# Soft mixture of experts behind pooled attention: scores by paired heads, one reader per output buffer, second engines in the last run

## The chip, the cores and the metric

One core of a Trainium2 chip runs the whole program. The time is device microseconds of one execution; lower is better. Three runs of the kernel before are known.

## The reference

```python
# attention: 8 batches, 8 heads, 576 tokens, head size 64; keys and values averaged over 8 neighbours
k_p, v_p = mean of 8 keys, mean of 8 values              # 72 per batch
attn = softmax(q @ k_p.T / 8) @ v_p                      # heads side by side: x is 4608 x 512
# dense layer with a rational function
h = x @ w_in                                             # 4608 x 2048
g = (a0 + a1*h + a2*h*h + a3*h*h*h) / (1 + |b0|*|h| + |b1|*h*h + 1e-6)
x = g @ w_out                                            # 4608 x 512
# soft mixture of 8 experts with 4 slots each
logits = x @ phi                                         # 4608 x 32
slot = softmax(logits, over tokens).T @ x                # 32 x 512
slot_out[e] = relu(slot[e] @ w1[e]) @ w2[e]              # 512 -> 1024 -> 512, each expert its 4 slots
out = softmax(logits, over slots) @ slot_out             # 4608 x 512
```

`w_in` and `w_out` arrive as float64, the rest as float32. The output is float32, 9.44 MB.

## The kernel before

**The work.** The 4608 tokens are 36 tiles of 128. Four tiles make a run, nine runs (r = 0 to 8) the dense part. `attention(t)` makes one tile of x: the scores of all eight heads against the 72 pooled keys (L364), VectorE's maximum and subtraction (L370, L374), the exponential on ScalarE, sums and normaliser, a multiplication (L389), eight transposes (`pt`, L398), the product with the pooled values (`av`, L409), and the split into a rounded part `xh` (ScalarE, L413) and the rest `xl` (VectorE, L414). `pooling(b)` sums a batch's keys into `kp` and its values into `vp` (L330, L337).

**Scores.** `kp` is [128, 4, 72]: head pair p, the even head in partitions 0 to 63 and the odd one in 64 to 127. Each head is a matmul of its own, of 64 rows and 72 columns, eight a tile; the even heads go to one PSUM buffer `sc`, the odd ones to another.

**Dense part.** `dense(r, p)` does two of the 16 F-tiles for the run's 512 tokens: h in one PSUM buffer of two banks, as three products of rounded words for each 128 rows of the contraction (L484 to L486). Then S=h*h, A=a3*h+a2 and U=|h| on ScalarE (L495, L497, L498); A=A*S on GpSimd (L499, tasks at L500), A=a1*h+A on VectorE (L502); S=b1*U+b0 and U=U*S on GpSimd (L505, L507); logarithm and negative exponential on ScalarE make the reciprocal r (L510, L513), in the single PSUM buffer `r`; three VectorE instructions (L514, L516, L518) refine it and multiply. TensorE adds this pair's logits (`lg`, L530) and transposes (`gp`, L534), and a copy puts the result into `gt` (L543). In run 0 the two multiplications may go to VectorE, and S to ScalarE. In the last run only the last pair is done in halves. `routing(r)` keeps the softmax over tokens running and adds the run's slot sums (`pss`, L593).

**Weights.** `win(f)` and `wout(f)` turn float64 words into float32 (`words`: one ScalarE instruction, L427, and three of VectorE, L428, L430, L432) during run 0; `win` splits them into `wh` (L441, L442), `wout` also makes w_out times phi by transposes (L454) into the buffer `wo` and a product (L463). So the logits need no x after the dense layer, and w_out is applied to the 32 slots alone at the end.

**End.** `experts()` issues 72 loads of 512 KB as buffers come free: eight of w_out, then w1 and w2. `tail()` applies w_out to the slots (L654), spreads them (`pi`, L663), multiplies by w1 (`l`, L708) and w2 (`lo`, L737), regroups (`pg`, L776), and combines: for each pair of tiles two products into one two-bank PSUM buffer `po` (L788), one half copied by ScalarE (L791), the other by VectorE (L793), both with the normaliser of the softmax over slots as scale, and one store of 512 KB (L795). Eighteen such pairs are there.

**The order.** Nothing is issued in the order of the code. Every instruction group is a task of `Plan` with an engine, a cost in the planner's units, a key (its due time) and buffers; some have a second engine as `alt`. `Plan.run` simulates the engines and gives out, at each step, the task that can start first, ties by key. HEAD, FIRST and RUN are the due times of the runs, SLACK the distance it keeps between a producer and TensorE. Engines then run their lists in order; semaphores hold what isn't ready.

## Time and profile before

| | us |
|---|---|
| three runs | 904.78, 908.6, 910.22; median 908.6 |
| the profiled execution | 908.17, of it 906.4 in the span |
| TensorE busy (share of the span) | 823.0 (91%) |
| VectorE, ScalarE, GpSimd busy | 622.7, 605.9, 523.5 |
| transferred | 97.60 MB |

The trace names TensorE PE (its weight loads PEld), VectorE DVE, ScalarE ACT, GpSimd POOL and the engine that issues the transfers SP. An fp32 matmul shows as two instructions. A line in square brackets gives the idle time ahead of an instruction and what ended it. The granted clock (PEclk) is 1.00 at TensorE's 2.4 GHz and 0.50 at its 1.2 GHz level. By stage: 0 to 55 us the first attention tiles, to 143 run 0, to 781 the h products of the other runs, to 811 the end of the last run, to 868 the experts, then the combine and its stores.

### The profile page before, as it was taken

To read this page: it belongs to the slowest core of one execution; us is meant where nothing else is said; L and a number is where in the kernel's file an instruction comes from. 1 tells how busy PE (TensorE), PEld (TensorE's weight loads), DVE (VectorE), ACT (ScalarE), POOL (GpSimd) and SP (SyncE) were. 2 spreads that over 40 slices of the span, in tenths; PEclk is the share of its full clock that TensorE was granted. 3 is DMA by queue.
4 is the path that set the end of the run, shared out by engine and by line. 5 is a ranking of instruction groups with operands and counts; after the bars stand their busy time and mean duration, and the time that the engine had idled before them with its cause. 6 is when DMAs were issued, how large, how long until landed. Compare 5 with 4: busy or idle time off the path is not lost.

```text
span 906.4 us, 15125 instructions
## 1 busy us (share of the span) xinstructions
PE 823.0 (91%) x5950; PEld 582.0 (64%) x5950; DVE 622.7 (69%) x978; ACT 605.9 (67%) x908; POOL 523.5 (58%) x333
## 2 busy tenths in 40 slices
PE   3778859799999999999999999999999999679987
PEld 3567637676777677677677767767777776433321
DVE  5888898946777777867887777758677667631023
ACT  2558757747888787788777868878877787731023
POOL 3225242856777778668866958667676766800000
PEclk9999869789999999999999999999999999869975
DMA  9694332240012100200130111000000443749947
GB/s 315 252 331 130 125 121 96 77 126 13 25 39 71 33 25 27 91 25 13 39 102 12 39 51 56 25 1 25 1 2 1 135 144 107 232 166 357 417 183 278
DMA packets 34151, 97.60 MB, mean 108 GB/s; under 512 B 3872, under 2 KB 4128, under 8 KB 34080
## 3 DMA queue, kind: packets, MB, share of 16 engines
q1 hardware_dynamic: 34080, 96.63, 31.1%
q8 instruction: 47, 0.77, 0.3%
q14 instruction: 24, 0.20, 0.1%
HBM read 82.99 MB, written 13.63 MB: 107 GB/s over the span
## 4 chain that ended last, share of the span: by engine, by line
PE 74%; DVE 12%; ACT 8%; DMA 2%; issue 2%; POOL 1%; SPq 0%; DVEq 0%; ACTq 0%; POOLq 0%
PE h L484 14%; PE h L486 13%; PE h L485 13%; PE gp L534 7%; PE av L409 4%; PE pss L593 4%; PE lg L530 4%; PE pt L398 3%; PE lo L737 3%; PE sc L364 3%; PE po L788 2%; DVE a L502 2%; PE l L708 2%; DVE r L516 2%; DVE u L514 1%
## 5 line engine op out<-in xcount | busy, mean ns | idle before, releaser
L484 PE MATMUL h<-xh,wh 128*128 128x512 f32 x576 | 249.5, 433 | 16.9 <-DVE a L502 8.6
L499 POOL TENSOR_TENSOR a<-a,s 128x1024 f32<-128x1024 f32 (+1 forms) x69 | 163.4, 2369 | 123.3 <-ACT a L497 112.9
L486 PE MATMUL h<-xh,wh 128*128 128x512 f32 x576 | 232.1, 403 | 0.5 <-POOL wh L442 0.3
L485 PE MATMUL h<-xl,wh 128*128 128x512 f32 x576 | 231.3, 402 | 0.0
L514 DVE SCALAR_TENSOR_TENSOR u<-u,r 128x512 f32<-128x512 f32 x144 | 98.2, 682 | 109.0 <-ACT r L513 105.3
L507 POOL TENSOR_TENSOR u<-u,s 128x1024 f32<-128x1024 f32 (+1 forms) x70 | 165.0, 2358 | 6.4 <-ACT s L504 1.2
L484 PEld LDWEIGHTS h<-xh,wh 128*128 128x128 f32 x576 | 111.4, 193 | 45.2 <-DVE a L502 12.3
L486 PEld LDWEIGHTS h<-xh,wh 128*128 128x128 f32 x576 | 111.0, 193 | 28.3 <-POOL wh L442 2.2
L485 PEld LDWEIGHTS h<-xl,wh 128*128 128x128 f32 x576 | 112.0, 195 | 18.1
L543 ACT ACTIVATE gt<-gp 128x512 f32<-128x512 f32 x143 | 79.8, 597 | 49.4 <-PE gp L534 47.9
L516 DVE SCALAR_TENSOR_TENSOR r<-a,abt,r 128x512 f32<-128x512 f32 x144 | 107.9, 749 | 0.0
L502 DVE SCALAR_TENSOR_TENSOR a<-h,abt,a 128x1024 f32<-128x1024 f32 (+1 forms) x73 | 92.2, 1264 | 20.1 <-POOL a L499 19.9
L518 DVE SCALAR_TENSOR_TENSOR a<-u,r 128x512 f32<-128x512 f32 x144 | 98.5, 684 | 4.3
L513 ACT ACTIVATE r<-s 128x512 f32<-128x512 f32 x144 | 86.8, 603 | 20.7 <-DVE a L518 19.8
L505 POOL TENSOR_SCALAR s<-u,gb 128x1024 f32<-128x1024 f32 (+1 forms) x71 | 84.4, 1188 | 16.3 <-DVE a L499 9.8
L498 ACT ACTIVATE u<-h 128x1024 f32<-128x1024 f32 (+1 forms) x73 | 73.7, 1011 | 26.1 <-PE h L486 25.7
L510 ACT ACTIVATE s<-u,cc 128x1024 f32<-128x1024 f32 (+1 forms) x73 | 83.2, 1140 | 6.9 <-POOL u L507 6.7
L497 ACT ACTIVATE a<-h,abt 128x1024 f32<-128x1024 f32 (+1 forms) x73 | 87.3, 1195 | 0.0
L534 PE MATMUL gp<-ident,a 128*128 128x128 f32 x576 | 84.0, 285 | 1.9 <-ACT cTs L587 1.1
L495 ACT ACTIVATE s<-h 128x1024 f32<-128x1024 f32 (+1 forms) x73 | 73.5, 1009 | 17.8 <-PE h L486 17.7
L534 PEld LDWEIGHTS gp<-ident,a 128*128 128x128 f32 x576 | 63.6, 143 | 22.0 <-issue 16.8
L389 POOL TENSOR_TENSOR at<-at,st 128x576 f32<-128x576 f32 x35 | 41.1, 1176 | 33.3 <-DVE st L383 29.7
(123 smaller groups left out, 1060.8 us busy)
## 6 DMA issues: line engine op xcount, KB each, us to landing
wx<-in_w SPq DMA_DIRECT2D x64, 512.0 KB
...
```

Source lines behind the costliest of these rows:

```text
L484: p_.matmul(o, w[:, 0, k], xh[r].t[:, k], start=(k == 0), stop=False)
L485: p_.matmul(o, w[:, 0, k], xl[r].t[:, k], start=False, stop=False)
L486: p_.matmul(o, w[:, 1, k], xh[r].t[:, k], start=False, stop=(k == 3))
L497: op("ACT", t_act(n, 1, 2), lambda fl=fl: a_.activation(out=fl(A), in_=fl(h), func=AF.Identity, scale=a3, bias=a2), [pt_(h), abt], [pt_(A) ...
L499: mul = lambda eng, fl=fl: eng.tensor_tensor(out=fl(A), in0=fl(A), in1=fl(S_), op=ALU.mult)
L502: op("DVE", t_dve(n, 1), lambda fl=fl: v_.scalar_tensor_tensor(out=fl(A), in0=fl(h), scalar=a1, in1=fl(A), op0=ALU.mult, op1=ALU.add), [pt ...
L507: mul = lambda eng, fl=fl: eng.tensor_tensor(out=fl(U), in0=fl(U), in1=fl(S_), op=ALU.mult)
L513: op("ACT", t_act(512, 0), lambda f=f, q=q: a_.activation(out=q.t, in_=S_.t[:, f], func=AF.Exp, scale=-1.0), [(S_, f)], [q], c + 10)
L514: op("DVE", t_dve(512), lambda f=f, q=q: v_.scalar_tensor_tensor(out=U.t[:, f], in0=U.t[:, f], scalar=QC, in1=q.t, op0=ALU.add, op1=ALU.mult),
L516: op("DVE", t_dve(512, 1), lambda f=f, q=q: v_.scalar_tensor_tensor(out=q.t, in0=A.t[:, f], scalar=a0, in1=q.t, op0=ALU.add, op1=ALU.mult) ...
L518: op("DVE", t_dve(512), lambda f=f, q=q: v_.scalar_tensor_tensor(out=A.t[:, f], in0=U.t[:, f], scalar=-2.0, in1=q.t, op0=ALU.add, op1=ALU. ...
L534: p_.transpose(pt.t[:, j, f, :], A.t[:, f, o : o + 128], ident)
```

## The change

- Scores: `kp` becomes block-diagonal, [128, 4, 144], zeroed once by GpSimd; key sums go to a buffer `ks` and two ScalarE copies put them into the blocks. One matmul of 128 rows and 144 columns makes both heads of a pair, four a tile, and `sc[0]` holds pairs 0 and 1. `av` reads `a` in the new order.
- Start and run 0: other due times, the queries of the first four tiles loaded first, all of run 0's multiplications on GpSimd (seven were on VectorE), six of its S on ScalarE instead of two, the weight transposes into `att` or `gt` instead of their own buffer.
- Last run: the last two pairs in halves; from pair 4 on the multiplications may go to VectorE, S to ScalarE, and r may take a `wk` buffer; A=a3*h+a2 may go to VectorE in all pairs; the copies of `gt` of the last two pairs too. The planner puts eight A (six whole, two halves) and one multiplication on VectorE there.
- Experts: items 28 and 29 are four half loads, three into query buffers and one into a score buffer; later items may use key and attention buffers. What is multiplied stays the same.
- Combine: the normaliser multiplies the 32 weights of each token ahead of their transposes (one VectorE instruction for each group of runs). Even pairs of tiles have one copy of 1024 columns, odd ones two PSUM buffers with a copy each, on whichever engine the planner finds free, without a scale.

```diff
-HEAD, FIRST, RUN = 30.0, 105.0, 75.0
+HEAD, FIRST, RUN = 27.6, 105.03, 75.0
...
-LAT, SLACK = 0.12, 0.6
+FINE, EITHER = 2, 4
+RW, GD, AD = 4, 6, 0
+A1, A1S = 26.91, 19.0
...
+E0 = 12
+LAT, SLACK = 0.12, 0.86
...
-                        s0 = max(s0, c[0] + LAT)
+                        s0 = max(s0, c[0] + LAT if c[0] else 0.0)
...
-                      ("t", 2, 512), ("wo", 1, 512)):
+                      ("t", 2, 512), ("ks", 1, 144)):
...
-    kp = [fixed([128, 4, SP], f"kp{i}", np_=2) for i in range(2)]
+    kp = [fixed([128, 4, 2 * SP], f"kp{i}", np_=2) for i in range(2)]
...
+        op("POOL", 0.75, lambda i=i: g_.memset(kp[i].t, 0.0), [], [kp[i]], -94)
...
-            return HEAD + 25 + 21.0 * j
+            return HEAD + A1 + A1S * j
...
-            o = kp[b % 2]
-            op("DVE", 1.35, lambda t=t, o=o, i=i: v_.tensor_reduce(out=o.t[:, 2 * i : 2 * i + 2, :], in_=t.t, axis=AX.X, op=ALU.add),
-               [], [t, (o, i)], key, alt=[("POOL", 2.8, lambda t=t, o=o, i=i: tree(t.t, o.t[:, 2 * i : 2 * i + 2, :]), True)] if b != 1 else ())
+            o = buf("ks", [128, 2, SP], "ks")
+            op("DVE", 1.35, lambda t=t, o=o: v_.tensor_reduce(out=o.t, in_=t.t, axis=AX.X, op=ALU.add),
+               [], [t, o], key, alt=[("POOL", 2.8, lambda t=t, o=o: tree(t.t, o.t), True)] if b > 1 or b == 0 and E0 & 8 else ())
+            for par in range(2):
+                rr = slice(64 * par, 64 * par + 64)
+                op("ACT", 0.33, lambda o=o, i=i, par=par, rr=rr: a_.activation(out=kp[b % 2].t[rr, 2 * i : 2 * i + 2, SP * par : SP * par + SP], in_=o.t[rr], func=AF.Copy),
+                   [o], [(kp[b % 2], i)], key + 0.1)
...
-        dma_in(q, lambda: q.t, qT[t], k0 - 30, 128 * 512 * 4)
+        dma_in(q, lambda: q.t, qT[t], (k0 if t > 3 else -8.2 + 0.1 * t) - 30, 128 * 512 * 4)
...
-                    for par in range(2):
-                        rr = slice(64 * par, 64 * par + 64)
-                        p_.matmul(sc[par].t[t0:t1, SP * p : SP * p + SP], q.t[rr, p, t0:t1], kp[bb % 2].t[rr, p, :], start=True, stop=True)
...
-        op("PE", 0.6 * len(sp_), scores, [q] + [kp[x % 2] for x in batches], sc, k0, also=[st, e])
+                    p_.matmul(sc[p // 2].t[t0:t1, 2 * SP * (p % 2) : 2 * SP * (p % 2) + 2 * SP], q.t[:, p, t0:t1], kp[bb % 2].t[:, p, :], start=True, stop=True)
...
+        op("PE", 1.0 + 0.2 * (len(sp_) - 1), scores, [q] + [kp[x % 2] for x in batches], sc, k0, also=[st, e])
...
-                        p_.matmul(av.t[64 * par : 64 * par + 64, p, t0:t1], vp[bb % 2].t[:, c : c + 64], a.t[:, par, p, t0:t1], start=True, stop=True)
+                        p_.matmul(av.t[64 * par : 64 * par + 64, p, t0:t1], vp[bb % 2].t[:, c : c + 64], a.t[:, p // 2, 2 * (p % 2) + par, t0:t1], start=True, stop=True)
...
-        wt = buf("wo", [128, 4, 128], "wt")
+        wt = buf(["att", "gt"], [128, 4, 128], "wt")
...
-        subs = [(0, 1), (1, 2)] if r == NR - 1 and p == NPAIR - 1 else [(0, 2)]
+        subs = [(0, 1), (1, 2)] if r == NR - 1 and p >= NPAIR - FINE else [(0, 2)]
+        either = r == 0 or r == NR - 1 and p >= EITHER
...
-            op("ACT", t_act(n, 1, 2), lambda fl=fl: a_.activation(out=fl(A), in_=fl(h), func=AF.Identity, scale=a3, bias=a2), [pt_(h), abt], [pt_(A)], c)
+            op("ACT", t_act(n, 1, 2), lambda fl=fl: a_.activation(out=fl(A), in_=fl(h), func=AF.Identity, scale=a3, bias=a2), [pt_(h), abt], [pt_(A)], c,
+               alt=[("DVE", t_dve(n, 1), lambda fl=fl: v_.tensor_scalar(out=fl(A), in0=fl(h), scalar1=a3, scalar2=a2, op0=ALU.mult, op1=ALU.add), False)] if r == NR - 1 and p >= AD else ())
...
-               alt=[("DVE", t_dve(n), lambda mul=mul: mul(v_), True)] if r == 0 else ())
+               alt=[("DVE", t_dve(n), lambda mul=mul: mul(v_), True)] if (E0 & 1 if r == 0 else either) else ())
...
-               [pt_(U), gb], [pt_(S_)], c + 4, alt=[wa] if r == 0 else ())
+               [pt_(U), gb], [pt_(S_)], c + 4, alt=[wa] if (E0 & 4 if r == 0 else either) else ())
...
-               alt=[("DVE", t_dve(n), lambda mul=mul: mul(v_), True)] if r == 0 else ())
+               alt=[("DVE", t_dve(n), lambda mul=mul: mul(v_), True)] if (E0 & 2 if r == 0 else either) else ())
...
-            q = buf("r", [128, 512], "r")
+            q = buf(["r", "wk"] if r == NR - 1 and p >= RW else "r", [128, 512], "r")
...
-               alt=[("DVE", 0.69, lambda gt=gt, gv=gv: v_.tensor_copy(gt.t[:, :, sl], gv()), False)] if r == NR - 1 and p == NPAIR - 1 else ())
+               alt=[("DVE", 0.69, lambda gt=gt, gv=gv: v_.tensor_copy(gt.t[:, :, sl], gv()), False)] if r == NR - 1 and p >= GD else ())
...
+            if 28 <= n < 30:
+                halves = [buf("q", [128, 512], "wx"), buf("q" if n == 28 else "at", [128, 512], "wx")]
+                w, e, k = it
+                v = lambda b: b.t if len(b.t.shape) == 2 else b.t.rearrange("p a h s -> p (a h s)")[:, 0:512]
+                for h, b in enumerate(halves):
+                    src = (w1 if w == 1 else w2)[e, k][:, 512 * h : 512 * h + 512]
+                    op("SP", 0.06, lambda b=b, src=src, v=v: nc.sync.dma_start(out=v(b), in_=src), [], [b], key, nbytes=128 * 2048)
+                ew[it] = (halves, lambda h, halves=halves, v=v: v(halves[h]))
+                continue
...
-                b = buf(["kv", "att"] if n < 8 else ["w", "gt", "A"], [128, 2, 512], "wx")
+                b = buf(["kv", "att"] if n < 8 else ["w", "gt", "A", "kv", "att"], [128, 2, 512], "wx")
...
+            op("DVE", t_dve(n), lambda c3=c3, cm=cm, nt=nt: v_.tensor_tensor(out=c3(), in0=c3(), in1=cm(2).rearrange("p (a o) -> p a o", o=1).to_broadcast([128, nt, 32]), op=ALU.mult),
+               [csum], [cr], kk, port=True)
...
-            po = buf("h", [128, 2, 512], "po", np_=2)
...
-            def comb(n=n, po=po):
+            po = [buf("h", [128, 2, DM], "po")] if n % 2 == 0 else [buf(["wk", "r"], [128, DM], "po") for _ in range(2)]
+            to = lambda i, po=po: po[0].t[:, i] if len(po) == 1 else po[i].t
...
+            def comb(n=n, to=to):
...
-                    p_.matmul(po.t[:, i], cTs.t[rr, n // 2, :], so4.t[rr, :], start=True, stop=True)
...
-            op("PE", 0.95, comb, [(cTs, n // 2), so4], [po], kk)
-            op("ACT", 0.69, lambda n=n, o=o, po=po: a_.activation(out=o.t[:, 0, :], in_=po.t[:, 0], func=AF.Copy, scale=csum.t[:, 2, 2 * n : 2 * n + 1]),
-               [(po, 0), csum], [(o, 0)], kk)
-            op("DVE", 0.75, lambda n=n, o=o, po=po: v_.tensor_scalar(out=o.t[:, 1, :], in0=po.t[:, 1], scalar1=csum.t[:, 2, 2 * n + 1 : 2 * n + 2], scalar2=None, op0=ALU.mult),
-               [(po, 1), csum], [(o, 1)], kk)
+                    p_.matmul(to(i), cTs.t[rr, n // 2, :], so4.t[rr, :], start=True, stop=True)
...
+            op("PE", 0.95, comb, [(cTs, n // 2), so4], po, kk)
+            for i in range(len(po)):
+                w = 2 * DM // len(po)
+                oo = lambda i=i, o=o, po=po: o.t if len(po) == 1 else o.t[:, i]
+                op("ACT", t_act(w), lambda i=i, oo=oo, po=po: a_.activation(out=oo(), in_=po[i].t, func=AF.Copy), [po[i]], [o if len(po) == 1 else (o, i)], kk,
+                   alt=[("DVE", t_dve(w), lambda i=i, oo=oo, po=po: v_.tensor_copy(oo(), po[i].t), False)])
```

**The order of the engines.** First VectorE in run 0, ahead of the `xl` of the 4th tile, before and after. `wi` and `wo` are words of w_in and w_out, `st` and `at` the softmax of a tile, L428 to L432 are L437 to L441 after.

```order
L428 TENSOR_SCALAR wi<-wi 128x512
L430 SCALAR_TENSOR_TENSOR wi<-raw,wi 128x512
L432 SCALAR_TENSOR_TENSOR wi<-raw,wi 128x512
L428 TENSOR_SCALAR wo<-wo 128x512
L430 SCALAR_TENSOR_TENSOR wo<-raw,wo 128x512
L370 TENSOR_REDUCE st<-sc 128x4
L374 TENSOR_TENSOR at_66<-sc,st 128x4x72 x2
L432 SCALAR_TENSOR_TENSOR wo<-raw,wo 128x512
L428 TENSOR_SCALAR wi<-wi 128x512
L430 SCALAR_TENSOR_TENSOR wi<-raw,wi 128x512
L432 SCALAR_TENSOR_TENSOR wi<-raw,wi 128x512
L414 SCALAR_TENSOR_TENSOR xl<-av,xh 128x4x128
```

```order
L379 TENSOR_REDUCE st<-sc 128x4 x2
L383 TENSOR_TENSOR at_66<-sc,st 128x4x72
L441 SCALAR_TENSOR_TENSOR wo<-raw,wo 128x512
L383 TENSOR_TENSOR at_66<-sc,st 128x4x72
L437 TENSOR_SCALAR wi<-wi 128x512
L439 SCALAR_TENSOR_TENSOR wi<-raw,wi 128x512
L423 SCALAR_TENSOR_TENSOR xl<-av,xh 128x4x128
```

Two `wi` and one or two `wo` conversions that stood ahead of the last `xl` are behind it now.

GpSimd at the end of the last run, before and after (`a`, `s`, `u` are A, S, U; x2 are two like rows; L499, L505, L507 are L510, L516, L518 after):

```order
L499 TENSOR_TENSOR a<-a,s 128x1024
L505 TENSOR_SCALAR s<-u,gb 128x1024
L507 TENSOR_TENSOR u<-u,s 128x1024
L499 TENSOR_TENSOR a<-a,s 128x512 x2
L505 TENSOR_SCALAR s<-u,gb 128x512 x2
L667 MEMSET sp 128x1024
L507 TENSOR_TENSOR u<-u,s 128x512 x2
L684 COPY selv<-sels 128x128
```

```order
L516 TENSOR_SCALAR s<-u,gb 128x1024
L518 TENSOR_TENSOR u<-u,s 128x1024
L510 TENSOR_TENSOR a<-a,s 128x512
L516 TENSOR_SCALAR s<-u,gb 128x512
L518 TENSOR_TENSOR u<-u,s 128x512
L510 TENSOR_TENSOR a<-a,s 128x512
L516 TENSOR_SCALAR s<-u,gb 128x512
L518 TENSOR_TENSOR u<-u,s 128x512
L687 MEMSET sp 128x1024
L510 TENSOR_TENSOR a<-a,s 128x512 x2
L516 TENSOR_SCALAR s<-u,gb 128x512
L518 TENSOR_TENSOR u<-u,s 128x512 x2
```

Pair 6 comes in halves of 512 columns as pair 7 does, and one of their `s` is no longer GpSimd's.

VectorE in the combine, with the semaphores that its copies wait for (DMAHW are transfers), before and after:

```order
L793 TENSOR_SCALAR o<-po,csum 128x512 [waits DMAHW3_49,DMAHW2_49,Activation_49]
L793 TENSOR_SCALAR o<-po,csum 128x512 [waits DMAHW4_49,Activation_49]
L793 TENSOR_SCALAR o<-po,csum 128x512 [waits DMAHW5_49,Activation_49]
L793 TENSOR_SCALAR o<-po,csum 128x512 [waits DMAHW6_49,Activation_49]
L793 TENSOR_SCALAR o<-po,csum 128x512 [waits DMAHW7_49,Activation_49]
```

```order
L818 COPY o<-po 128x512 [waits DMAHW2_49,PE_49]
L818 COPY o<-po 128x512 [waits DMAHW4_49,PE_49]
L818 COPY o<-po 128x512 [waits DMAHW5_49,DMAHW2_49,PE_49]
L818 COPY o<-po 128x512 [waits DMAHW7_49,DMAHW4_49,PE_49]
L818 COPY o<-po 128x512 [waits DMAHW6_49,DMAHW1_49,PE_49]
```

The copies waited for ScalarE (Activation); they wait for TensorE (PE) now. There were 18 of them, there are 9.

## Rows read from the trace of the kernel before

**Rows 1.** Page, the chain that ended last: share of the span by engine.
```profile
PE 74%; DVE 12%; ACT 8%; DMA 2%; issue 2%; POOL 1%; SPq 0%; DVEq 0%; ACTq 0%; POOLq 0%
```

**Rows 2.** Windows by stage: busy us per engine (instructions), granted clock, DMA share and GB/s.
```profile
core 0: us, PE busy (x) PEld busy (x) DVE busy (x) ACT busy (x) POOL busy (x), PEclk, DMA share, GB/s
90.00:130.00 40.00, 31.40 (x190) 23.83 (x192) 35.44 (x56) 26.95 (x43) 15.85 (x12) 0.74 0.32 101
...
450.00:525.00 75.00, 72.49 (x578) 54.93 (x580) 57.33 (x93) 58.95 (x88) 57.06 (x37) 1.00 0.16 47
...
750.00:806.00 56.00, 42.27 (x293) 29.27 (x285) 36.98 (x56) 37.85 (x60) 33.19 (x20) 0.84 0.52 169
```

**Rows 3.** Timeline of TensorE (start us, us, instruction); last, scores' weight loads by form.
```profile
488.91 0.40 PE L486 MATMUL h<-xh,wh 128*128 128x512 f32 x1
489.24 1.12 PE L364 MATMUL sc<-kp,qt 64*128 64x72 f32 x16
490.28 0.50 PE L484 MATMUL h<-xh,wh 128*128 128x512 f32 x1
...
504.34 0.39 PE L486 MATMUL h<-xh,wh 128*128 128x512 f32 x1
504.57 1.03 PE L398 MATMUL pt<-ident,at 128*72 128x128 f32 x8
505.37 0.47 PE L484 MATMUL h<-xh,wh 128*128 128x512 f32 x1
...
818.75 1.08 PE L663 MATMUL pi<-sels,sS 128*128 128x32 f32 x8 [0.71 <-ACT sS L658]
...
L364 PEld LDWEIGHTS sc<-kp,qt 64*128 64x128 f32 x512 | 35.8, 205 | 24.2 <-issue 20.0 <-ACT r L513 1.8 <-ACT a L401 0.8
```

**Rows 4.** Run 0: timeline; lines by form (busy us, mean ns of one | idle before).
```profile
49.62 1.98 PE L409 MATMUL av<-a,vp 72*64 72x128 f32 x16 [5.96 <-DVE at L374]
...
55.06 0.77 PE L484 MATMUL h<-xh,wh 128*128 128x512 f32 x1
...
L430 DVE SCALAR_TENSOR_TENSOR wo<-raw,wo 128x512 int32<-128x512 int32 x16 | 15.2, 947 | 0.5
...
L430 DVE SCALAR_TENSOR_TENSOR wi<-raw,wi 128x512 int32<-128x512 int32 x16 | 11.1, 692 | 0.5
...
L499 DVE TENSOR_TENSOR a<-a,s 128x1024 f32<-128x1024 f32 x4 | 5.0, 1249 | 5.6 <-ACT a L497 5.6
...
115.19 2.50 POOL L499 TENSOR_TENSOR a<-a,s 128x1024 f32<-128x1024 f32 x1 [3.44 <-ACT a L497]
...
115.51 2.73 DVE L430 SCALAR_TENSOR_TENSOR wo<-raw,wo 128x512 int32<-128x512 int32 x1
```

**Rows 5.** End of the last run: timeline; TensorE's waits from 750 to 806 (total, times, longest).
```profile
780.67 2.39 POOL L499 TENSOR_TENSOR a<-a,s 128x1024 f32<-128x1024 f32 x1 [3.34 <-ACT s L495]
...
781.20 0.39 PE L486 MATMUL h<-xh,wh 128*128 128x512 f32 x1
...
806.00 4.94 PE L593 MATMUL pss<-gt,en 128*32 128x512 f32 x32 [0.37 <-ACT en L586]
...
PE lg L530 <- DVE a L518: 10.4, 6, 2.8
```

**Rows 6.** Window in the second expert product, columns as in rows 2.
```profile
858.00:862.00 4.00, 4.00 (x15) 1.16 (x14) 0.00 (x0) 0.00 (x0) 0.00 (x0) 1.00 1.03 420
```

**Rows 7.** The combine: lines by form, timeline, and one window.
```profile
L791 ACT ACTIVATE o<-po,csum 128x512 f32<-128x512 f32 x18 | 12.3, 687 | 20.0 <-PE po L788 20.0
...
L788 PE MATMUL po<-so,cTs 32*128 32x512 f32 x72 | 27.2, 1062 | 4.7 <-DVE o L793 3.7 <-DVE so L778 0.9
...
872.85 30.22 SPq L795 DMA_DIRECT2D out_dram<-o  x18
...
876.38 0.75 DVE L793 TENSOR_SCALAR o<-po,csum 128x512 f32<-128x512 f32 x1 [0.51 <-ACT o L791]
...
874.00:878.00 4.00, 3.69 (x12) 1.05 (x10) 1.50 (x2) 1.37 (x2) 0.00 (x0) 0.50 0.96 351
```

17 lines of the change are left out of this document (9 added, 8 removed).

## The prediction

> **What bounds the kernel now.** I read the chain that ended last first: TensorE holds 74% of it and VectorE 12% [rows 1], so a saved microsecond counts where TensorE runs without a gap, or where it waits for something the change touches. The windows by stage [rows 2] tell these apart. In a middle run (450 to 525) TensorE is busy 72.49 of 75 us at full clock; there only less TensorE work helps. In 90 to 130 (run 0) VectorE is busy 35.44 of 40 us and TensorE 31.40 at a granted clock of 0.74 of full: VectorE, which converts the weights' words, sets the pace. In 750 to 806 (end of the last run) every engine has gaps, TensorE 13.7 us of them: a chain through several engines bounds it. After that come the experts' weights, bound by their transfers, and the combine. The sum is made against the profiled execution, 908.17 us (span 906.4), which lies 0.4 us under the median, 908.6.
>
> **1. Start and run 0.** Here the row with the longest wait is TensorE's at 49.62: 5.96 us for VectorE's score subtraction of the 4th tile; the first h product follows at 55.06 [rows 4]. The new order puts seven conversion instructions fewer on VectorE ahead of the 4th tile's `xl` (68 arithmetic instructions there before, 61 after). An L430 takes 0.69 or 0.95 us on the mean [rows 4]; the three kinds have the same size, and I take 0.6 each: about 4 us earlier for the first h. Against it: seven of run 0's multiplications were on VectorE (four L499 at 1.25 us and three L507 of the same size), and all go to GpSimd, where one took 2.50 us [rows 4]; VectorE is relieved of 7 x 1.25 = 8.7 us, GpSimd gets 7 x 2.50 = 17.5 us, less four S that go to ScalarE. GpSimd is busy only 15.85 of 40 us there [rows 2], so there is room. But the conversions that moved back have to be done before their F-tile anyway, and the key copies (144 columns; between nothing and the 0.69 us of a 512-column copy in [rows 7], I take 0.3) go to ScalarE, four at each of the early loads, where it is busy 26.95 of 40 us: hidden. I take -3.5 us, between -11 (first h 4 us earlier and 7 of VectorE's 8.7 us of relief) and +7 (rival B).
>
> The rows at 115 us also show a collision: a conversion (L430) that started during GpSimd's multiplication took 2.73 us, and the L430 rows of `wo` have a mean of 947 ns beside 692 for `wi` [rows 4]. The Trainium skill, "SBUF — State Buffer" (section "SBUF: two separate sides"), says that VectorE and GpSimd share a port pair that is held for a whole instruction, so that the other blocks fully. This trace agrees (2.73 us for a 0.69 us instruction). It speaks against moving multiplications to GpSimd, and is rival B's mechanism.
>
> **2. Scores.** One group before lies between two h products: the last h matmul before starts at 488.91, the first after it at 490.28, so the group costs TensorE 1.37 us for its 16 instructions (8 fp32 matmuls of 64 rows by 72 columns, two instructions each) [rows 3]. After it is 4 matmuls, 8 instructions, of 128 rows by 144 columns. No row shows that shape. Nearest: the transposes `pt`, 8 instructions of 128 rows and 128 columns, take 504.57 to 505.37 = 0.80 us, with 0.23 us ahead of them (504.34 to 504.57); and `pi`, 128-row weights of 128 columns with only 32 columns moving, 8 in 1.08 us with its pipeline's end [rows 3]. That `pi` costs about as much as `pt` says the weight load (128 columns) is what an instruction costs at least, and that it lies beside the moving data. I take 0.11 us x 144/128 = 0.124 us an instruction: 0.23 + 8 x 0.124 + 0.03 = 1.25 us, -0.12 us a group. The 28 tiles of runs 2 to 8 are scored during runs 1 to 7, some 25 of them where TensorE bounds: -3 us. The cheap end (0.80/8 x 144/128 = 0.113 each, no gap but 0.23) gives 1.13, -6 us; the dear end is an unhidden load, which gives rival A.
>
> The Trainium skill, "TensorEngine Tiling (Array Packing)" (section "Theoretical Speedup"), says that contractions of 64 rows or fewer gain up to 2x by packing two into the array, which the old scores do and the new ones give up. By that rule nothing is gained: half as many instructions of twice the columns cost the same 1.37 us, and the sum would be 3 us higher. The rows can't tell how much of the packing the old 16 instructions reached: 0.065 us each against 0.10 for a `pt` instruction of 1.8 times the columns.
>
> **3. Middle runs otherwise.** The order is planned anew with later due times for work that feeds TensorE. TensorE idles only 2.5 of 75 us there [rows 2]: bounds -5 to +5 over seven runs; I take 0. The weight transposes lose their own buffer, but `att` and `gt` have eleven.
>
> **4. End of the last run.** TensorE's last h product starts at 781.20, the slot product `pss` at 806.00: 24.8 us of chain [rows 5]. GpSimd starts pair 6's multiplication at 780.67 after 3.34 us of waiting for ScalarE's square, and has one more pair behind it; TensorE waits 10.4 us, six times, for VectorE's last product `a` [rows 5]. After, pair 6 is in halves too, so GpSimd can begin after one F-tile of h instead of two; the first form a3*h+a2 may run on VectorE while ScalarE squares, and the reciprocal may use either of two kinds of PSUM buffer. GpSimd's work from pair 6 on stays the same but for one s of a half (four a, three s, four u at half size); one multiplication of pair 5 goes to VectorE. So the gain is in its earlier start: its 3.34 us of wait, and something for the `r` buffer: -4 us. Bounds: 0, if VectorE, which has u, r and a in this chain, is the next late one; -7 if both waits go.
>
> **5. Expert weights.** At the end of the last run (750 to 806) the DMA engines are 0.52 busy at 169 GB/s [rows 2], with loads waiting for free buffers, though 1.03 busy at 420 GB/s later [rows 6]. Two more items (1 MB, 1,048,576 B at 420 GB/s = 2.5 us) start early into the query and score buffers, and later ones may use the key and attention buffers. As the transfers bound the expert stage, what is loaded early shortens it: 2.5 us, plus up to 2 us of gap, with the earlier end of the run in part 4 starting the stage earlier too: -4 us. Bounds 0 (the transfers are delayed elsewhere) and -4.6.
>
> **6. Combine.** Before, VectorE's copy waits for ScalarE's of the same buffer (idle 0.51 us in the row shown), and only then is the buffer free: a loop of 0.69 + 0.75 us and the two products, with TensorE busy 3.69 of 4 us at a granted clock of 0.50, its 1.2 GHz level. The 18 stores are under way 30.22 us from 872.85 on [rows 7], 3.4 us for 4 tiles. After, an even pair has one reader (ScalarE, 1024 columns) and an odd pair two buffers of 512, one to each engine, and the copies wait for TensorE alone. ScalarE needs at most 3 x 0.69 = 2.1 us for 4 tiles and VectorE 0.75, far below 3.4. What is late next is the transfer: 351 GB/s in the 4 us where DMA was 0.96 busy [rows 7] makes 366 GB/s; 9.44 MB take 25.8 us, some 4.4 us less than 30.22, and the first store leaves some 0.4 us earlier. The extra multiplication by the normaliser lies beside the expert products. I take -5. Bounds -8 (TensorE at full clock, stores at 420 GB/s) and -2.5: at half clock the 36 products, busy 27.2 us [rows 7], may stay the bound, at 27.2/9 = 3.0 us for 4 tiles and more where they don't overlap.
>
> **Sum.** -3.5 - 3 + 0 - 4 - 4 - 5 = -19.5: 908.17 - 19.5 = 888.7, forecast 889 us.
>
> **Rivals.**
> A. The weight loads of the 128-row scores are exposed. If no load of such a group lies beside the moving data, each of 8 instructions costs its load (0.205 us, the mean of today's 128-column score loads, [rows 3]) and its 0.124 us: 0.23 + 8 x 0.329 = 2.86 us, +1.49 a group, +37 us over 25. With the other 16.5 us won that is 908.17 + 37 - 16.5 = 929: slower. It decides from 2.03 us a group (1.37 + 16.5/25) on. For it: no 144-column fp32 product is in the trace. Against: `pt` runs at 0.10 an instruction with loads beside it. Chance 0.07.
> B. GpSimd's seven added multiplications lock VectorE out. If each holds one conversion up by 2.73 - 0.69 = 2.04 us, that is +14.3 us of VectorE's time less the 8.7 relieved, and the gain of 3.5 us at the start becomes about +5: 908.17 - 16 + 5 = 897. For it: the rows at 115 us. Against: only some conversions meet a multiplication. Chance 0.15.
> C. The ends don't give. The chain of the last run moves to VectorE (0), the transfers then start earlier but end with the same bytes (-1), and the combine stays with TensorE at half clock (-2.5): 908.17 - 3.5 - 3 - 3.5 = 898. For it: TensorE's 3.69 of 4 us in the combine. Against: the alternation of the two engines is plain in the rows. Chance 0.2.
>
> **How the numbers follow.** The forecast and its neighbours (880 to 894) get 0.5, A 0.07, B 0.15, C 0.2; 0.08 is left for better ends together (below 880). A measurement of this kernel tells about 1% from no change, so faster means below 899.5, slower above 917.7. Faster: 0.5 + 0.08 + 0.12 of B + 0.1 of C = 0.8, less 0.02 for what I have missed: 0.78. Same: the rest of B and C, and the light form of A: 0.15. Slower: 0.07. The range from 876 (all terms near their better ends, not all at once) to 903 (C with B's lock) holds 8 in 10.
>
> **What would show it.** Right: a score group of 8 instructions between two h products in 1.1 to 1.3 us; the first h product near 51; GpSimd's last pair done near 788, `pss` near 795 on the new scale; stores near 360 GB/s, with the DMA share over 0.9 from the first to the last. Wrong: score groups over 1.5 us; VectorE's conversions with means over 1 us beside GpSimd; the expert products waiting as long for their weights; TensorE still 90% busy at half clock in the combine.

## The result and the profile after

The changed kernel takes 881.4 us in the median of four runs (877.6 to 883.71) beside 906.69 us of the kernel before: a ratio of 0.9714, 95% interval 0.9662 to 0.9765, 25 us faster. The forecast was 889, in a range of 876 to 903. The profiled execution took 880.67 us, its span 878.9; against the 908.17 that the sum was made from, 27.5 us are gone in this pair of profiles, where the sum had 19.5.

Where they went is read from a few starts in both timelines: the first h product of runs 0, 1, 2 and 8, the last run's slot product `pss`, the spreading product `pi`, the first product `po` of the combine, and the end of the span.

| start, us | before | after | difference | gained since the row above |
|---|---|---|---|---|
| first h product, run 0 | 55.06 | 48.01 | -7.05 | 7.05 |
| run 1 | 179.01 | 176.79 | -2.2 | -4.8 |
| run 2 | 260.29 | 254.60 | -5.7 | 3.5 |
| run 8 | 716.77 | 706.50 | -10.3 | 4.6 |
| last run's `pss` | 806.00 | 790.65 | -15.4 | 5.1 |
| `pi` | 818.75 | 804.58 | -14.2 | -1.2 |
| first `po` | 870.18 | 849.64 | -20.5 | 6.4 |
| end | 906.4 | 878.9 | -27.5 | 7.0 |

How sure are single rows? The kernels of e2, e3, e4 and e8 below have, up to run 1, the changed kernel's order of instructions on every compute engine. In these five traces the first h product stands at 48.0 to 50.6 us and run 1's at 174.0 to 176.8, so the first row is 4.5 to 7 us, and 2 to 5 us are won by run 1's start. The 3.5 us of the row of run 2 belong mostly to TensorE's clock: in the trace of before run 1 began at the 1.2 GHz level (0.50 up to 187 us), and with the old scores at 1.00 it takes 77.1 us (e1). Run 1, then runs 2 to 7, each before and after (columns as in [rows 2]):

```profile
179.01:260.29 81.28, 80.74 (x616) 61.42 (x614) 50.65 (x86) 56.19 (x83) 52.03 (x36) 0.95 0.15 46
176.79:254.60 77.81, 76.78 (x565) 58.58 (x562) 59.23 (x93) 60.31 (x89) 51.60 (x29) 1.00 0.17 49
...
260.29:716.77 456.48, 448.57 (x3527) 335.47 (x3527) 344.25 (x546) 359.65 (x526) 338.32 (x201) 1.00 0.11 35
254.60:706.50 451.90, 445.98 (x3345) 338.83 (x3343) 339.96 (x543) 363.92 (x543) 346.67 (x210) 1.00 0.12 37
```

Of the 4.6 us of runs 2 to 7, TensorE has 2.6 us less work and 2.0 us less idle time.

The chain of the page and three windows by stage (us, busy and instructions of PE, PEld, DVE, ACT, POOL; granted clock, DMA share, GB/s), to be held against [rows 1, 2]:

```profile
PE 73%; DVE 9%; ACT 8%; DMA 4%; issue 2%; POOL 2%; SPq 0%; ACTq 0%; DVEq 0%; POOLq 0%
```

```profile
90.00:130.00 40.00, 30.02 (x208) 24.84 (x208) 34.03 (x46) 27.50 (x48) 18.41 (x12) 0.80 0.41 135
450.00:525.00 75.00, 74.38 (x564) 56.46 (x563) 59.14 (x96) 60.29 (x92) 62.47 (x42) 1.00 0.15 47
735.00:790.00 55.00, 46.02 (x314) 31.34 (x313) 46.24 (x67) 36.63 (x62) 33.77 (x23) 0.87 0.51 177
```

VectorE has less of the chain (9% for 12%) and the transfers more (4% for 2%). Run 0 looks as it did, the middle runs are TensorE's as before, and in the 55 us ahead of `pss` TensorE is idle 9 us where it was 13.7.

**Scores.** The timeline of TensorE (start, us, instruction), a group between two h products in run 2, and the scores' weight loads by form:

```profile
303.62 0.39 PE L495 MATMUL h<-xh,wh 128*128 128x512 f32 x1
303.85 1.14 PE L373 MATMUL sc<-kp,qt 128*128 128x144 f32 x8
304.74 0.49 PE L493 MATMUL h<-xh,wh 128*128 128x512 f32 x1
...
L373 PEld LDWEIGHTS sc<-kp,qt 128*128 128x128 f32 x256 | 37.6, 201 | 18.7 <-issue 9.5 <-ACT gt L554 3.4 <-ACT wt L467 1.4
```

From h product to h product are 1.12 us (the median of 23 such groups from run 1 on; the longest takes 2.02) where [rows 3] has 1.37. Of the 0.25 us, 0.10 lie ahead of the group: its first instruction starts 0.23 us after the last h product, with 64 rows 0.33 us. The weight loads are as long as before (201 ns by the records), so they lie beside other instructions: 8 x 0.201 would be more than the group.

**Start and run 0.** Timeline of TensorE ahead of the first h product, and conversions by form (busy us, mean ns):

```profile
42.57 1.98 PE L418 MATMUL av<-a,vp 72*64 72x128 f32 x16 [2.46 <-DVE at L383]
...
48.01 0.77 PE L493 MATMUL h<-xh,wh 128*128 128x512 f32 x1
...
L439 DVE SCALAR_TENSOR_TENSOR wo<-raw,wo 128x512 int32<-128x512 int32 x16 | 11.9, 744 | 0.5
...
L437 DVE TENSOR_SCALAR wi<-wi 128x512 int32<-128x512 int32 x16 | 9.6, 603 | 0.4 <-ACT wi L436 0.4
```

The wait for VectorE's subtraction is 2.46 us where it was 5.96, and h starts 7 us earlier in this trace [rows 4]. Collisions with GpSimd moved (the second `wo` form is down from 947 to 744 ns, the first `wi` form up from 419 to 603 ns), and the six forms take 66.1 us in all where they took 64.6. Run 0 ends with the attention of the eighth token tile, which run 1 needs. VectorE's last instruction of it, `xl`, marks its place, in the trace of the kernel before and after:

```profile
175.56 0.68 DVE L414 SCALAR_TENSOR_TENSOR xl<-av,xh 128x512 fp32r<-128x512 f32 x1
```

```profile
174.94 0.68 DVE L423 SCALAR_TENSOR_TENSOR xl<-av,xh 128x512 fp32r<-128x512 f32 x1
```

It moved by 0.6 us only: of the 7 us at the start run 0 gives 4.8 back. TensorE didn't wait for `xl` itself (run 1's first h product follows 2.8 us after its end before, 1.2 us after it now); what holds the whole tile there isn't shown.

**End of the last run.** Timeline of GpSimd and TensorE, then TensorE's waits from 735 on (total, times, longest), then windows:

```profile
770.56 1.30 POOL L518 TENSOR_TENSOR u<-u,s 128x512 f32<-128x512 f32 x1
...
771.83 0.40 PE L495 MATMUL h<-xh,wh 128*128 128x512 f32 x1
...
777.53 2.50 POOL L518 TENSOR_TENSOR u<-u,s 128x512 f32<-128x512 f32 x2
...
790.65 6.10 PE L604 MATMUL pss<-gt,en 128*32 128x512 f32 x32 [0.37 <-ACT en L597]
...
PE gp L545 <- ACT gt L554: 4.3, 2, 2.9
PE lg L541 <- DVE a L529: 1.3, 2, 0.9
...
784.00:788.00 4.00, 3.08 (x22) 1.85 (x17) 1.47 (x5) 0.92 (x3) 0.00 (x0) 0.50 0.69 249
788.00:792.00 4.00, 2.62 (x12) 1.19 (x16) 0.89 (x4) 1.94 (x8) 0.00 (x0) 0.50 0.33 115
...
804.00:808.00 4.00, 3.11 (x28) 1.74 (x32) 0.22 (x1) 0.75 (x2) 0.00 (x0) 1.00 1.02 413
```

When the last h products run, GpSimd has pair 6 behind it; from the last h product to `pss` are 18.8 us where [rows 5] has 24.8. The wait for VectorE's `a` is down from 10.4 to 1.3 us, but 4.3 us of wait for ScalarE's copies into `gt` are new. From `pss` to `pi` 1.2 us are lost: `pss` lies at 0.50 and takes 6.10 us, in [rows 5] 4.94. The transfers still starve (0.33 busy from 788 to 792), but from 796 on they run without a gap.

**Combine.** Timeline, one window, and lines by form:

```profile
851.87 21.40 SPq L819 DMA_DIRECT2D out_dram<-o  x18
...
855.35 1.51 ACT L817 ACTIVATE o<-po 128x512 f32<-128x512 f32 x2 [0.30 <-PE po L811]
855.45 0.69 DVE L818 COPY o<-po 128x512 f32<-128x512 f32 x1 [1.12 <-PE po L811]
856.00 1.14 PE L811 MATMUL po<-so,cTs 32*128 32x512 f32 x8 [0.67 <-ACT o L817]
...
858.00:862.00 4.00, 2.67 (x24) 0.74 (x21) 1.39 (x2) 3.41 (x5) 0.00 (x0) 1.00 1.04 390
...
L811 PE MATMUL po<-so,cTs 32*128 32x512 f32 x72 | 11.1, 635 | 6.4 <-ACT o L817 5.4 <-DVE so L800 0.9
```

The row of ScalarE holds two copies, of 1024 and of 512 columns. No copy waits for the other engine. Four tiles take TensorE 1.14 us and a round 1.81 us; the products are done at 866, and the stores alone run on, 1.03 busy; in windows of 4 us from 854 on they move 378 to 408 GB/s. TensorE kept its 2.4 GHz level here, where [rows 7] shows 0.50.

### The profile page after: what moved, and what is told of

Its sections match the earlier page's. It is cut to its first block, busy times and chain, and to the rows that moved or that the text cites. A ratio compares the mean times of both kernels' runs of the same rounds, so it can differ in the third digit from the quotient of the medians.

```text
span 878.9 us, 14545 instructions
## 1 busy us (share of the span) xinstructions
PE 794.9 (90%) x5630; PEld 578.6 (66%) x5630; DVE 622.0 (71%) x976; ACT 614.0 (70%) x941; POOL 534.6 (61%) x336
## 4 chain that ended last, share of the span: by engine, by line
PE 73%; DVE 9%; ACT 8%; DMA 4%; issue 2%; POOL 2%; SPq 0%; ACTq 0%; DVEq 0%; POOLq 0%
PE h L493 14%; PE h L495 13%; PE h L494 13%; PE gp L545 7%; PE pss L604 4%; PE lg L541 4%; PE av L418 4%; PE lo L757 3%; PE pt L407 3%; PE sc L373 2%; DVE a L513 2%; DMA raw<-in_w_in 2%; PE l L728 2%; PE pw L472 1%; ACT u L509 1%
## 5 line engine op out<-in xcount | busy, mean ns | idle before, releaser
L510 POOL TENSOR_TENSOR a<-a,s 128x1024 f32<-128x1024 f32 (+1 forms) x73 | 171.6, 2351 | 129.4 <-ACT a L507 107.4
L518 POOL TENSOR_TENSOR u<-u,s 128x1024 f32<-128x1024 f32 (+1 forms) x74 | 173.0, 2339 | 7.9 <-ACT s L515 2.6
L505 ACT ACTIVATE s<-h 128x1024 f32<-128x1024 f32 (+1 forms) x74 | 74.0, 1000 | 36.5 <-PE h L495 34.4
L524 ACT ACTIVATE r<-s 128x512 f32<-128x512 f32 x144 | 86.8, 603 | 10.3 <-DVE a L529 9.0
L545 PE MATMUL gp<-ident,a 128*128 128x128 f32 x576 | 87.0, 290 | 4.8 <-ACT gt L554 4.3
L516 POOL TENSOR_SCALAR s<-u,gb 128x1024 f32<-128x1024 f32 (+1 forms) x67 | 79.4, 1186 | 9.6 <-DVE a L510 2.9
L545 PEld LDWEIGHTS gp<-ident,a 128*128 128x128 f32 x576 | 65.4, 146 | 24.3 <-issue 13.7
L507 ACT ACTIVATE a<-h,abt 128x1024 f32<-128x1024 f32 (+1 forms) x66 | 78.8, 1194 | 0.0
L373 PE MATMUL sc<-kp,qt 128*128 128x144 f32 (+1 forms) x320 | 47.0, 310 | 14.9 <-ACT kp L341 7.4
```

The costliest lines, as they stand in the source:

```text
L510: mul = lambda eng, fl=fl: eng.tensor_tensor(out=fl(A), in0=fl(A), in1=fl(S_), op=ALU.mult)
L518: mul = lambda eng, fl=fl: eng.tensor_tensor(out=fl(U), in0=fl(U), in1=fl(S_), op=ALU.mult)
L524: op("ACT", t_act(512, 0), lambda f=f, q=q: a_.activation(out=q.t, in_=S_.t[:, f], func=AF.Exp, scale=-1.0), [(S_, f)], [q], c + 10)
L545: p_.transpose(pt.t[:, j, f, :], A.t[:, f, o : o + 128], ident)
```

## The experiments

Twelve kernels, each against the kernel before on the same chip. Medians below are to be held against the changed kernel's 881.4 us and its ratio of 0.9714, whose interval is some 5 us to either side: a difference of 3 or 4 us in the medians alone doesn't show. The stretch from run 8's first h product to the end is steadier: the kernels with all new ends and the new distance take 170.1 to 173.4 us for it in their profiles, the changed one 172.4. The edits are shortened; the text names what is left out.

### One part undone

**Scores of 64 rows.**

```diff
-                    p_.matmul(sc[p // 2].t[...], q.t[:, p, t0:t1], kp[bb % 2].t[:, p, :], ...)
+                    for par in range(2):
+                        p_.matmul(sc[par].t[...], q.t[rr, p, t0:t1], kp[bb % 2].t[rr, p, :], ...)
```

(Also back: key sums straight into `kp` without copies, the order of `a`, and the planner's cost of a group, 0.6 for 1.0.)

> The changed kernel with the old scores (64 rows by 72 columns, one matmul a head, key sums straight into kp) and all else kept. Theory: the pair form saves 1.37 - 1.11 = 0.26 us in each score group where TensorE bounds, some 25 groups, so this kernel is 5 to 7 us slower than the changed one (about 887, ratio to before 0.978), the groups between two h products back at 1.37 us. Rival (the old form reached the same rate and the middle runs gained from the new order alone): within 2 us of the changed kernel, ratio 0.971.

897.77 us, ratio 0.9895 (0.9873 to 0.9916): 16 us slower, more than either theory said. In the middle runs (run 1's first h product to run 8's) it takes 537.9 us beside 529.7, 8 us, and the groups are back at 1.37 us. The other 9 us come at the start: the first h product stands at 57.1, run 1's at 185.9. Two rows of this kernel, run 1 and TensorE ahead of the first h product:

```profile
185.91:263.02 77.11, 76.31 (x607) 59.40 (x605) 53.93 (x84) 58.91 (x88) 50.44 (x28) 1.00 0.11 34
```

```profile
50.88 1.98 PE L414 MATMUL av<-a,vp 72*64 72x128 f32 x16 [5.90 <-DVE at L379]
```

Run 1 is as short with the old scores, at 1.00, as with the new. In runs 2 to 7 TensorE idles 5.3 us more than in the changed kernel, and twice its clock is at 0.50 for some 3 us (0.59 and 0.57 in 274 to 278 and 370 to 374). At the start the first tiles' scores lie on TensorE's chain, at its 1.2 GHz level (2.73 us a group in the timeline; 2.26 in the changed kernel at that level), and with their other cost the planner orders VectorE differently: the wait of 5.90 us is back. So the 16 us hold the price of another order too, and not that of the groups alone. The rival fell.

**The combine as before.**

```diff
-            po = [buf("h", [128, 2, DM], "po")] if n % 2 == 0 else [buf(["wk", "r"], [128, DM], "po") for _ in range(2)]
+            po = buf("h", [128, 2, 512], "po", np_=2)
```

(The normaliser is the copies' scale again, and each pair has one copy on either engine.)

> The changed kernel with the old combine (two readers in turn on one PSUM buffer, normaliser as scale in the copies). Theory: the alternation of ScalarE and VectorE holds TensorE up and the stores with it; the stretch from the first combine product to the end goes from 29.3 back to about 36 us, 7 us slower than the changed kernel (about 888, ratio 0.979), with the granted clock at 0.50 in that stretch. Rival (the stretch is shorter because TensorE happened to keep its clock or because the stores found a freer memory): 29 to 31 us, ratio 0.972.

886.93 us, ratio 0.9801 (0.9776 to 0.9826): 5.5 us slower by the medians, 8 by the ratios (0.0087 x 906.6). The last stretch takes 37.1 us, near the theory's 36, and from run 8's start to the end are 181.4 us. Timeline and windows of this kernel:

```profile
857.01 1.41 DVE L813 TENSOR_SCALAR o<-po,csum 128x512 f32<-128x512 f32 x2 [2.24 <-ACT o L811]
...
858.00:862.00 4.00, 3.08 (x10) 1.32 (x12) 1.76 (x3) 1.34 (x2) 0.00 (x0) 0.50 0.70 262
```

The alternation is back, the stores run at 262 GB/s in this window and TensorE at its 1.2 GHz level. All 14 traces agree: from the first to the last product of the combine the granted clock is 0.51 to 0.58 in the mean in the four with the old form, and 0.90 to 1.00 in the ten with the new. So the clock goes with the form of the combine and wasn't chance; which of the two, clock or alternation, holds the loop longer was not tried apart.

**The experts' loads as before.**

```diff
-            if 28 <= n < 30:
...
-                b = buf(["kv", "att"] if n < 8 else ["w", "gt", "A", "kv", "att"], [128, 2, 512], "wx")
+                b = buf(["kv", "att"] if n < 8 else ["w", "gt", "A"], [128, 2, 512], "wx")
```

> The changed kernel without the four half loads into query and score buffers and without reuse of key and attention buffers for later loads. Theory: the experts' weights bound the stretch from the spreading product to the combine, and each megabyte loaded ahead is 2.5 us: that stretch goes from 45.1 to 47.6 to 51 us, 2.5 to 6 us slower in all (about 885, ratio 0.975 to 0.978). Rival (the stretch got shorter because the last run ended with less idle time, so the same loads started sooner): within 1 us of the changed kernel, ratio 0.972.

884.53 us, ratio 0.9757 (0.9735 to 0.9779): 3.1 us slower. `lo` to the combine takes 34.4 us where all kernels with the new buffers take 28 to 29.5. Windows of this kernel:

```profile
788.00:792.00 4.00, 3.67 (x20) 0.92 (x24) 1.50 (x6) 0.75 (x4) 0.00 (x0) 0.57 0.00 0
...
804.00:808.00 4.00, 4.00 (x41) 1.40 (x35) 0.00 (x0) 0.00 (x0) 0.00 (x0) 1.00 0.59 178
```

The transfers stand still at 788 and starve once more at 804, where the changed kernel has 1.02. The medians' 3.1 us lie within the intervals, but the stretch from run 8's first h product to the end, 176.8 us, is 4.4 us longer than in the changed kernel and clear of the others; the spreading product to the combine takes 50.8. The theory holds. It is more than the 2.5 us of the two items; what of it the reuse of key and attention buffers gives was not tried apart.

**The last run as before.**

```diff
-FINE, EITHER = 2, 4
-RW, GD, AD = 4, 6, 0
+FINE, EITHER = 1, 8
+RW, GD, AD = 8, 7, 8
```

> The changed kernel with the last run as before: only the last pair in halves, no second engines for its multiplications, S, A or copies, r only in its own PSUM buffer. Theory: the stretch from the last h product to the slot product goes from 19.3 back to about 25 us; the weights' transfers bound what follows, so of these 6 us only the part that delays buffers shows at the end: 3 to 6 us slower (885 to 887, ratio 0.975 to 0.978). Rival (the transfers hide all of it): the stretch is 6 us longer but the end within 1 us of the changed kernel, ratio 0.972.

885.82 us, ratio 0.9763 (0.9737 to 0.9788): 4.4 us slower. Timeline of this kernel:

```profile
771.60 2.39 POOL L510 TENSOR_TENSOR a<-a,s 128x1024 f32<-128x1024 f32 x1 [4.75 <-ACT a L507]
...
797.06 2.79 PE L604 MATMUL pss<-gt,en 128*32 128x512 f32 x12 [0.37 <-ACT en L597]
```

GpSimd starts pair 6 at 771.60, after 4.75 us of waiting; TensorE's wait for `a` is back (10.3 us); `pss` comes 6.4 us later than in the changed kernel, and the end 6.2 us later in the profile (178.9 us from run 8's start, clear of the others). In the profile the transfers hide none of it, and the rival fell.

**Run 0's multiplications on VectorE again.**

```diff
-E0 = 12
+E0 = 15
```

> The changed kernel with run 0's multiplications allowed on VectorE again (the planner takes seven there, as before). Theory (VectorE sets run 0's pace and GpSimd has room): run 1's first h product comes later than the 174 to 177 us of the kernels that keep them on GpSimd, by 2 to 5 us, total 884 to 886, ratio 0.975 to 0.977. Rival (GpSimd's multiplications lock VectorE's conversions out, so the move cost what it saved): run 1 starts at 174 or earlier, ratio 0.967 to 0.972.

884.29 us, ratio 0.9736 (0.9713 to 0.9759), within the changed kernel's interval. Run 1 starts at 176.9 us, as in the changed kernel (176.8). Neither theory: VectorE, busy 111.4 us instead of 103.7 from the first h product to run 1, doesn't delay it by anything beyond the spread, and the conversions take 66.4 us in all with seven multiplications fewer on GpSimd and 66.1 with them, so the move has no price there either. The eighth tile's `xl` stands where it stood (174.60).

**All old due times; the old distance alone; run 1's attention alone.** Three kernels: HEAD, FIRST, A1, SLACK and the queries' keys as before; SLACK alone; A1 and A1S alone. HEAD and FIRST alone leave the order of the compute engines as it is; three early loads change places.

```diff
-HEAD, FIRST, RUN = 27.6, 105.03, 75.0
-A1, A1S = 26.91, 19.0
-LAT, SLACK = 0.12, 0.86
+HEAD, FIRST, RUN = 30.0, 105.0, 75.0
+A1, A1S = 25, 21.0
+LAT, SLACK = 0.12, 0.6
```

> The changed kernel with the old due times (HEAD, FIRST, run 1's attention, SLACK, the query loads' keys). Theory (the order ahead of the 4th tile gives the early start): first h product at 53 to 56 us instead of 48 to 50, and run 1's start 2 to 5 us later; total 884 to 887, ratio 0.975 to 0.978. Rival (the shorter score groups give the early start, the due times nothing): first h product at 48 to 50 us, ratio 0.970 to 0.973.

> The changed kernel with the old distance between a producer and TensorE (SLACK 0.6), all other due times new. Theory (of the 20 us that all old due times cost together, 13 to 15 lie in run 0 and come from this distance, which sets when conversions stand ahead of other work): run 1 starts at 185 to 192 us, total 890 to 897, ratio 0.982 to 0.989. Rival (run 1's attention keys and the query loads are the cause): within 3 us of the changed kernel, ratio 0.971 to 0.975.

> The changed kernel with the old keys of run 1's attention (21 us apart instead of 19, the last some 4 us later), all other due times new. Theory (the distance to TensorE is the cause of what old due times cost): within 3 us of the changed kernel, ratio 0.970 to 0.975. Rival (the last attention tile of run 1 comes too late): run 1 starts 3 to 10 us later, at 179 to 187 us, ratio 0.975 to 0.983.

All old: 901.46 us, ratio 0.9929 (0.991 to 0.9948), 20 us slower; the first h product at 54.4 us is as the theory said, run 1's at 192.0 is 15 us later and not 2 to 5. SLACK alone: 898.62 us, 0.9902 (0.9877 to 0.9928), 17 us slower. Run 1's attention alone: 880.35 us, 0.9708 (0.9683 to 0.9732), no difference, though in its profile run 1 starts at 181.3. With the old distance the first h product is still early (49.5 us), but run 1 starts at 191.4. Timeline of that kernel:

```profile
171.52 0.80 PE L493 MATMUL h<-xh,wh 128*128 128x512 f32 x1 [3.07 <-ACT wh L450]
...
189.86 0.69 DVE L423 SCALAR_TENSOR_TENSOR xl<-av,xh 128x512 fp32r<-128x512 f32 x1 [1.62 <-ACT xh L422]
```

The eighth tile's `xl` comes 15 us later than in the changed kernel. So the distance, not the keys, decides run 0: it sets how far ahead of TensorE its producers stand, and with the shorter one the eighth tile's attention comes last. With all old due times the last word of w_in is late as well (its GpSimd subtraction starts at 181.90). What in the order would have to stand where was not tried.

### The scores' rate

**The same columns in twice the instructions.**

```diff
-                    p_.matmul(sc[p // 2].t[...], q.t[:, p, t0:t1], kp[bb % 2].t[:, p, :], ...)
+                    for par in range(2):
+                        p_.matmul(sc[p // 2].t[..., c : c + SP], q.t[:, p, t0:t1], kp[bb % 2].t[:, p, SP * par : SP * par + SP], ...)
```

> The changed kernel with each pair's matmul of 128 rows by 144 columns cut into two of 128 rows by 72 columns: the same columns in all, twice the instructions and weight loads. Theory (a weight load of 128 columns sets the least time of an instruction): a group between two h products takes 0.23 + 16 x 0.11 = 2.0 us instead of 1.11, the kernel is some 20 us slower than the changed one (about 901, ratio 0.994). Rival (moving columns set it, 0.11 x 72/128 an instruction): 1.1 to 1.3 us a group, ratio 0.972 to 0.977.

901.14 us, ratio 0.9927 (0.9905 to 0.9949), 20 us slower, as the theory said. Timeline of this kernel:

```profile
311.81 0.39 PE L497 MATMUL h<-xh,wh 128*128 128x512 f32 x1
312.04 1.90 PE L375 MATMUL sc<-kp,qt 128*128 128x72 f32 x16
313.74 0.48 PE L495 MATMUL h<-xh,wh 128*128 128x512 f32 x1
```

A group takes 1.93 us: less the 0.23 us ahead, 16 instructions at 0.106. The changed kernel's 8 take (1.12 - 0.23)/8 = 0.111, for twice the columns. So an instruction with 128 columns of weights costs 0.11 us whether 72 or 144 columns move: the load, lying beside the moving data of the one before, sets the rate. A fixed price of every instruction would show the same in these rows; the tiles that span two batches speak against it, whose weights are 64 columns wide. In the changed kernel and in this one:

```profile
423.69 1.20 PE L373 MATMUL sc<-kp,qt 128*64 128x144 f32 x16
```

```profile
436.65 1.27 PE L375 MATMUL sc<-kp,qt 128*64 128x72 f32 x32
```

To the next h product they take 1.13 and 1.20 us, 0.07 and 0.04 an instruction: less than 0.11, and here the columns decide. These groups didn't gain: from h product to h product they take 1.46, 1.46 and 1.59 us in the changed kernel, and took 1.30, 1.34 and 1.59 before. The old instructions of 64 rows took (1.37 - 0.33)/16 = 0.065 each, two in 0.13: by this estimate packing two into the array gave 0.106 x 2/0.13 = 1.6 times the rate, and one matmul for two heads gives 0.106 x 2/0.111 = 1.9 times.

### One part alone

**Pair scores on the kernel before.**

```diff
-                    for par in range(2):
-                        rr = slice(64 * par, 64 * par + 64)
-                        p_.matmul(sc[par].t[...], q.t[rr, p, t0:t1], kp[bb % 2].t[rr, p, :], ...)
+                    p_.matmul(sc[p // 2].t[...], q.t[:, p, t0:t1], kp[bb % 2].t[:, p, :], ...)
```

(With the block-diagonal `kp`, its copies, the buffer of the transposed weights, and the planner's cost of a group, as in the changed kernel.)

> The kernel before with the pair scores alone (block-diagonal keys, ScalarE's copies, 4 matmuls of 144 columns; the transposed weights in the score or gate buffers, since the wider keys need the room of their own buffer); its due times and all other parts as before. Theory (the pair form saves 0.26 us a group in the middle runs whatever the due times, while the start needs both): run 1's first h product to run 8's 529 to 532 us instead of 537.8, run 1's start not earlier than before's 179, total 898 to 902 (ratio 0.989 to 0.995). Rival (the pair form alone gives the early start too): run 1 starts at 175 to 177 us, ratio 0.985 or less.

908.08 us, ratio 1.0005 (0.9987 to 1.0022): no gain at all. Run 1 starts 2.3 us earlier, the groups take 1.12 us, and yet the middle runs take 538.1 us, as before. TensorE's waits from run 2's to run 8's start, in this kernel and before:

```profile
PE h L489 <- DVE a L507: 10.0, 10, 2.3
```

```profile
PE h L484 <- DVE a L502: 5.8, 9, 1.6
```

What the groups save goes into other things: the h products wait 4.2 us more for VectorE, which reads the h bank last (L507). Besides, TensorE's clock is twice at 0.50 for some 3 us in these runs, where runs 2 to 7 of the kernel before show 1.00 as a whole:

```profile
467.00:471.00 4.00, 4.00 (x16) 3.07 (x14) 3.06 (x4) 3.32 (x5) 3.90 (x3) 0.57 0.37 94
590.00:594.00 4.00, 4.00 (x13) 2.82 (x12) 3.24 (x6) 3.70 (x8) 2.70 (x2) 0.58 0.00 0
```

So the planner, with the groups' new cost but the old distance, finds an order in which waits and clock take the gain. Neither theory held.

**The due times on the kernel before.**

```diff
-LAT, SLACK = 0.12, 0.6
+LAT, SLACK = 0.12, 0.86
```

(and HEAD, FIRST, A1, A1S and the queries' keys of the changed kernel)

> The kernel before with the new due times alone (HEAD, FIRST, run 1's attention, SLACK, query loads first). Theory (the due times were fitted to the pair scores and give nothing by themselves, as the changed kernel with 64-row scores had its first h product at 57.1): first h product at 54 to 58 us, within 4 us of before, ratio 0.996 to 1.004. Rival (the order they give is better by itself): first h product near 50 and run 1 4 us earlier, ratio 0.985 to 0.993.

911.32 us, ratio 1.0046 (1.0026 to 1.0065): slower by 4 to 5 us, a little beyond the theory's range. First h product at 56.7 us, run 1 at 177.9. By themselves the due times gain nothing, as the theory said.

### One step further

**Another item ahead.** The two buffers of 512 columns for words are idle after run 0; one more item goes into them.

```diff
-            if 28 <= n < 30:
-                halves = [buf("q", [128, 512], "wx"), buf("q" if n == 28 else "at", [128, 512], "wx")]
+            if 28 <= n < 31:
+                halves = [buf("t" if n == 30 else "q", [128, 512], "wx"), buf({28: "q", 29: "at", 30: "t"}[n], [128, 512], "wx")]
```

> The changed kernel with one more expert item (512 KB) loaded ahead, as two halves into the two word buffers that are idle after run 0. Theory (transfers bound the experts' stage and buffers bound the transfers): 524,288 B at 420 GB/s = 1.2 us less in the stretch to the combine, total about 880, ratio 0.970. Rival (something else ends last there): no difference, ratio 0.9714.

877.94 us, ratio 0.9673 (0.9647 to 0.9699). `lo` to the combine takes 27.9 us, 0.8 less than in the changed kernel's profile and 0.9 to 1.5 less than in the others with the new buffers, which differ among themselves by 0.6. It has the lowest median of all, but its interval overlaps the changed kernel's, so the 3.5 us between the medians aren't shown; some 1 us in the stretch fits the theory's 1.2.

## Why the prediction was right

The sign, the size and the range held, and no rival did. By the steps:

1. **Start and run 0, -3.5.** At run 1's start 2 to 5 us are won. The first half of the step held: conversions went behind the fourth tile, the wait for VectorE shrank by 3.5 us, and h starts 4.5 to 7 us earlier, not 4; the shorter scores on the same chain were left out of the step, and it takes both (57.1 us with the old scores, e1; 54.4 with the old due times, e6). The second half failed: "VectorE is relieved of 7 x 1.25 = 8.7 us" brought nothing (e5, with the multiplications back, starts run 1 at the same time). Run 0 ends with the eighth tile's attention, which hardly moved. The sum came near by luck.
2. **Scores, -3.** The size is right by two errors that cancel. A group gained 0.25 us and not 0.12: the step scaled an instruction with its columns (0.11 x 144/128) although `pi` [rows 3] with 32 columns cost about as much as `pt` with 128; from 72 to 144 columns the load sets the rate. But not 25 groups gained that. The 22 that lie between two h products in runs 2 to 7 take 33.8 us before, 4.0 of it waits, and 27.9 after, 1.4 of it waits: 3.4 us less work, since the tiles that span two batches gained nothing and some others less. Run 1's 3.5 us are mostly the clock's and not the scores' (e1). The Trainium skill, "TensorEngine Tiling (Array Packing)" ("Theoretical Speedup"), gives up to 2x for packing; by the estimate from e7 the packed form reached 1.6 here, so the rival drawn from it, no gain, didn't come.
3. **Middle runs otherwise, 0.** The net is near 0, but the step took the planner's numbers for harmless. SLACK alone is worth 17 us with the new parts, mostly in run 0, and all new due times together gain nothing with the old parts (e10).
4. **End of the last run, -4.** 5.1 us to `pss`, 3.9 to `pi`: GpSimd's earlier start was as written, and e4 gives 4.4 us back by the medians. What the `r` buffer and the second engines each give was not tried apart. The next late one is ScalarE with its copies into `gt` (4.3 us), which the step didn't name.
5. **Expert weights, -4.** 6.4 us in the profile. e3 gives 5.7 back in the stretch and 3.1 at the end: the bound of 4.6 allowed too little for the transfers' gaps, which e3 shows at 804 and the changed kernel does not.
6. **Combine, -5.** 7.0 us. The loop was as written; stores ran at 378 to 408 GB/s and not at 366, and TensorE stayed at 2.4 GHz, which stood at the far bound. e2 gives 7.9 back in the stretch, 5.5 at the end.

Rival A (exposed loads): the loads set the rate but lie beside the data; 1.12 us a group. Rival B (locks): e5 shows no price of the move. Rival C (the ends don't give): each end gave. Of the signs, the groups (1.12 us) and the first h product came as named; GpSimd's last pair is done at 780.0, `pss` stands at 790.7 and the stores run at 378 to 408 GB/s, all beyond what was named.

The parts don't add. Undoing each alone costs 16 (scores), 17 to 20 (due times), 5.5, 3.1 and 4.4 us, 46 to 49 together, while all give 25; and scores or due times alone on the kernel before give nothing. The prediction added terms, and its first three are one: an order fitted to these durations. What in that order makes run 0 shorter stays open.
